# A gated MLP behind linear attention on one core: batches 0 and 1 share a tile for their last 64 positions, in a new order of steps

## The chip, the cores and the metric

The kernel runs on one core of one Trainium2 chip. The metric is device time in microseconds of one execution, taken as the median of several runs. The engines are called PE (TensorE, matmuls; PEld is its weight load), DVE (VectorE), ACT (ScalarE), POOL (GpSimd) and SP (SyncE, which here only issues loads and stores).

## What is computed

For each of 8 batches (8 heads, 576 positions, 64 channels a head) a linear attention, whose output x has 576 positions of 512 channels, and behind it a gated MLP. Cut to what matters:

```python
q_s = softmax(q, axis=-1); k_s = softmax(k, axis=2)
kv = einsum('bhsd,bhse->bhde', k_s, v)
x = einsum('bhsd,bhde->bhse', q_s, kv)          # then (b, s, 512)
h = gelu(x @ w_in)                              # 512 -> 1024
u, v = h[..., :512], h[..., 512:]
v_n = (v - mean(v)) / sqrt(var(v) + 1e-6) * g_ln
v_s = einsum('ts,bsd->btd', w_sg, v_n) + b_sg   # over the 576 positions
out = x + (u * v_s) @ w_out
```

## The kernel before, in words

Every matrix operand that meets another in the MLP is split into a high and a low part (names ending in h and l: x_h and x_l, wi_h and wi_l, ws_h and ws_l, vnh and vnl), and a product is the sum of three products of parts. One batch b passes through these steps, each a function of the kernel:

- load_q, load_k, load_v; the softmax of q (q_max, q_swapm, q_top, q_sub, q_exp, q_sum, q_swapd, q_inv, q_mul) and its transpose (q_turn); the maximum over positions of k (k_ma, k_mb, k_mc, k_fold, k_rota, k_maxa, k_rotb, k_maxb), k_sub and k_exp. Batch 0 has steps of its own for some of this (names qf_ and kr_).
- kv_mm, kv_inv, kv_scale, and x by x_mm (batch 1, line 660), xf_mm (batch 0) or xm_mm (batches 2 to 7, line 706); the copies x_high, xm_high, xt_high on ACT make the high part, x_low, xm_low, xt_low the low part. xt is the tail, the last 64 positions.
- hv_mm b i (line 773): the v half of the first layer for a tile of 128 positions, 12 matmuls of 512 columns; hv_gelu, hv_sq, hv_stat, hv_pow, hv_norm and then hv_high, hv_low give the normalized parts. i = 4 is the tail tile.
- hu_mm b f (line 843): the u half, 24 matmuls of 288 columns; hu_gelu.
- sg_mm b d (line 860): the product with w_sg, 28 matmuls of 288 columns, the last four of them with the tail (vn_1, vn_2); gate, gate_high, gate_low.
- out_mm b e: the last layer, 24 matmuls; out_base (x_h + x_l), out_add, out_store. The last one of batch 7 is done in halves (last_mm).

The 576 positions are four tiles of 128 and a tail of 64. For batches 2 to 7 an even batch and the odd one after it share one tail tile: hv_mm of the even batch with i = 4 holds both tails, and the odd batch writes its tail into the even batch's x as well (second, line 34; x_places, line 744; tail_places, line 727; tail, line 823). To have that tail in columns 0 to 63, the positions of odd batches are turned on the host so that the tail comes first, and w_sg and b_sg are laid out with 640 columns, the tail's both in front and behind; halves takes an offset (line 656 on). Batches 0 and 1 stand in ALONE (line 27): each has a tail tile of 64 positions of its own, so hv_mm 0 4 and hv_mm 1 4 both exist, each with 64 rows.

The weights are converted once at the start from raw 64-bit words: wi_a, wi_b, wi_c, wi_d, wi_h, wi_l for the eight pieces of w_in, the same with wo_ for w_out, ws_h and ws_l for w_sg, b_h and b_l for b_sg. hv_mm needs pieces 4 to 7 of w_in. Steps called warm are matmuls without use that keep PE at work at the start.

What sets the order: PLAN (line 39) is a list of all steps, written out, and the kernel runs through it once (line 921). Every engine's own instructions, SP's loads and stores among them, stay in the order of the list (InOrder, and mm for PE); across engines only data and buffers order them. A trailing V, G or A in a step says which engine does it: DVE, POOL or ACT. Buffers are slots taken in turn: two for k (kk) and q (qq), one pair for v (vv), four for v after the gelu, two banks of one kind of PSUM tile for hv_mm, kv_mm and the tails and three of a wider kind for the rest. So load_k b h can be issued once kv_mm of the batch before, same h, has read its slot, and SP's later loads and stores wait behind it.

Two quoted pieces say how x and the tail tile are addressed:

```python
def rows(b, i):
    return slice(0, TL if i == ST and b in ALONE else P)
...
        yield ps2_of(b, p)[:, :, 0:HS], split(whole(x, b)[:, p, 0:S])
        if second(b):
            yield ps2_of(b, p)[:, 0, 0:TL], x(b - 1)[:, p, S:S + TL]
```

Of the kernel before, what the change touches and what calls it, by code (L numbers as in the profile page):

```python
# [63 lines left out]
k_ma 2 1, k_mb 2 1, hv_pow 0 2, hv_high 0 2, hv_stat 0 4 A, hv_norm 0 4, hv_pow 0 4, tail_high 0, tail_again 0, ws_l 4 G, hv_stat 1 3 A, ws_h 3
k_mc 2 1, hv_mm 1 1, hv_pow 1 3, k_fold 2 1, k_rota 2 1, hv_sq 1 0, load_q 2 0, wo_h 3, load_k 2 0, q_max 2 0, q_swapm 2 0, hv_low 0 2, ws_l 3 V
tail_low 0, sg_mm 0 3, hv_gelu 1 2, k_ma 2 0, k_mb 2 0, wo_l 2 V, q_top 2 0, k_mc 2 0, k_fold 2 0, k_rota 2 0, k_maxa 2 1, k_rotb 2 1, gate 0 3
q_sub 2 0 G, hv_norm 1 3, hv_gelu 1 1 A, hv_sq 1 1, k_maxb 2 1, sg_mm 0 0, gate 0 0, wo_l 3 G, k_maxa 2 0, sg_mm 0 1, hv_stat 1 2, k_sub 2 1 V
# [4 lines left out]
q_turn 2 1, load_k 3 0, load_v 3 0, out_mm 0 1, hv_pow 1 0, kv_inv 2 1, wo_h 0, wo_l 0 G, q_sub 2 1 G, out_base 0 2 V, out_add 0 2, out_base 0 3 V
out_add 0 3, q_mul 2 0 0 G, q_turn 2 0, out_mm 0 0, q_exp 2 1, q_sum 2 1, q_swapd 2 1, out_base 0 1 G, out_add 0 1, hu_mm 1 2, k_ma 3 0, k_mb 3 0
k_mb 3 1, k_mc 3 0, q_inv 2 1, load_q 3 0, out_base 0 0 G, out_add 0 0, q_mul 2 1 1 V, out_store 0 0, hu_gelu 1 2, k_mc 3 1, hu_mm 1 3, hu_gelu 1 3
kv_scale 2 1, q_mul 2 1 0 G, q_turn 2 2, out_store 0 3, k_fold 3 0, k_rota 3 0, q_turn 2 3, xm_mm 2, k_fold 3 1, k_rota 3 1, q_max 3 0, xt_high 2
# [904 lines left out]
```

## Time and profile before

| | |
|---|---|
| median of 3 runs | 496.66 us (495.96 to 496.99) |
| profiled execution, span | 495.2 us, 9520 instructions |
| PE busy | 482.7 us, 97% |
| DVE busy | 356.0 us, 72% |
| ACT busy | 286.0 us, 58% |
| POOL busy | 177.3 us, 36% |
| HBM read, written | 37.64 MB, 9.44 MB |

The span runs from the first to the last instruction of the one execution that the profiler recorded; it is 1.46 us below the median of the runs, which were timed apart, and no other time is given for the profiled execution. The busy times are averages over stages with different limits. Nearly all operations of DVE, ACT and POOL have one line in the profile (164, the helper that keeps the order), and all matmuls have line 253, so rows are told apart by tiles, shapes and time.

### The profile page before, as it was taken

How to read it: one execution, taken by the hardware profiler on the slowest of the kernel's cores; microseconds unless marked ns; L12 is line 12 of the kernel's file. 1: busy time of each engine (PE TensorE's matmuls, PEld its weight loads, DVE VectorE, ACT ScalarE, POOL GpSimd, SP SyncE). 2: the span in 40 equal slices, each digit the busy share in tenths (PEclk: the TensorE clock that was granted, in tenths of full speed). 3: DMA queues.
4: the chain of work that ended last, by engine and by line, in shares of the span. 5: the costliest groups of instructions: out<-in, count | busy, mean ns of one | idle time of the engine just before them, and what ended most of it. 6: DMA issues, size and time to landing. Idle time of an engine off the chain costs nothing.

```text
span 495.2 us, 9520 instructions
## 1 busy us (share of the span) xinstructions
PE 482.7 (97%) x3859; PEld 444.3 (90%) x3859; DVE 356.0 (72%) x610; ACT 286.0 (58%) x603; POOL 177.3 (36%) x136
## 2 busy tenths in 40 slices
...
GB/s 316 388 396 132 190 136 1 157 141 100 1 94 207 82 16 49 107 29 116 97 66 134 119 46 34 1 72 196 8 2 1 144 73 1 1 0 49 1 1 144
DMA packets 16303, 47.68 MB, mean 96 GB/s; under 512 B 1922, under 2 KB 3332, under 8 KB 16260
## 3 DMA queue, kind: packets, MB, share of 16 engines
q1 hardware_dynamic: 16112, 47.01, 27.0%
...
HBM read 37.64 MB, written 9.44 MB: 95 GB/s over the span
## 4 chain that ended last, share of the span: by engine, by line
PE 82%; DVE 9%; DMA 3%; ACT 2%; issue 2%; SPq 1%; POOL 0%; DVEq 0%; ACTq 0%; POOLq 0%
PE ps L253 82%; DVE ot_i L164 2%; DVE km L164 1%; DMA qq<-q 1%; DVE qd L164 1%; DMA vv<-v 1%; DVE qm L164 1%; SPq L164 1%; DVE o L164 1%; DMA qq<-q_flat 1%; DVE kf L164 1%; ACT L164 1%; DVE qq L164 0%; ACT v L164 0%; POOL o L164 0%
## 5 line engine op out<-in xcount | busy, mean ns | idle before, releaser
L164 POOL TENSOR_TENSOR rs<-ve,half 128x1 f32<-128x1 f32 (+1 forms) x37 | 30.4, 826 | 101.4 <-DVE ve L164 101.4
L253 PE MATMUL ps<-ulow,wo_h 128*128 128x288 f32 x256 | 55.5, 296 | 0.0
L253 PE MATMUL ps<-gh,wo_h 128*128 128x288 f32 x256 | 55.5, 295 | 0.0
L253 PE MATMUL ps<-gh,wo_l 128*128 128x288 f32 x256 | 55.3, 295 | 0.0
L253 PE MATMUL ps<-ws_h,vnh 128*128 128x288 f32 x256 | 55.2, 297 | 0.0
L253 PE MATMUL ps<-ws_l,vnh 128*128 128x288 f32 x256 | 54.9, 296 | 0.0
L253 PE MATMUL ps<-ws_h,vnl 128*128 128x288 f32 x256 | 54.9, 296 | 0.0
L164 POOL TENSOR_TENSOR ulow<-u,gh 128x576 fp32r<-128x576 f32 x17 | 28.0, 1645 | 66.5 <-ACT gh L164 55.8
L164 POOL TENSOR_TENSOR qq<-qq,qm 128x1152 f32<-128x1152 f32 (+2 forms) x13 | 26.5, 2040 | 62.7 <-DVE qm L164 42.9
L164 ACT ACT_TABLE_LOAD x34 | 43.6, 1283 | 7.5 <-issue 3.6
L164 DVE TENSOR_TENSOR u<-ps,u 128x576 f32<-128x576 f32 x32 | 23.9, 750 | 32.8 <-PE ps L253 32.7
L164 ACT CAST gh<-u 128x576 fp32r<-128x576 f32 x32 | 21.2, 670 | 43.5 <-DVE u L164 43.5
L253 PEld LDWEIGHTS ps<-ws_h,vnh 128*128 128x128 f32 x256 | 41.5, 188 | 0.8
L253 PEld LDWEIGHTS ps<-gh,wo_h 128*128 128x128 f32 x256 | 41.3, 188 | 0.6
L253 PE MATMUL ps<-wi_h,x_h 128*128 128x512 f32 (+1 forms) x148 | 41.0, 398 | 0.7 <-DVE x_l L164 0.7
L253 PE MATMUL ps<-x_h,wi_h 128*128 128x288 f32 (+2 forms) x256 | 40.7, 299 | 0.7 <-ACT x_l L164 0.7
L253 PEld LDWEIGHTS ps<-gh,wo_l 128*128 128x128 f32 x256 | 41.3, 188 | 0.0
L253 PEld LDWEIGHTS ps<-ws_h,vnl 128*128 128x128 f32 x256 | 41.1, 188 | 0.0
L253 PEld LDWEIGHTS ps<-ulow,wo_h 128*128 128x128 f32 x256 | 41.1, 188 | 0.0
L253 PEld LDWEIGHTS ps<-ws_l,vnh 128*128 128x128 f32 x256 | 41.0, 188 | 0.0
L253 PE MATMUL ps<-wi_h,x_l 128*128 128x512 f32 (+1 forms) x148 | 40.9, 396 | 0.0
L253 PE MATMUL ps<-wi_l,x_h 128*128 128x512 f32 (+1 forms) x148 | 40.5, 395 | 0.0
...
## 6 DMA issues: line engine op xcount, KB each, us to landing
...
```

The lines of the kernel that those rows point to most:

```text
L164: ins = op(*args, **kw)
L253: tc.keep_in_program_order(nc.tensor.matmul(*args, **kw))
```

## The change

ALONE becomes empty: batches 0 and 1 share one tail tile, hv_mm 0 4 with 128 rows, and hv_mm, hv_gelu, hv_stat, hv_norm and hv_pow of 1 4 leave the plan. Batch 1 writes its tail into batch 0's x as well, so its x_high and x_low have one more copy each. The positions of odd batches keep their order, w_sg and b_sg have 576 columns, and halves loses its offset. The list of steps is in another order from end to end; 69 steps change between DVE and POOL. The number of warm steps stays eight, and no other step comes or goes (1259 steps before, 1254 after).

```diff
-WT = S + TL
+WT = S
...
-ALONE = [0, 1]
+ALONE = []
...
-    def halves(z, o=0):
-        return [z[..., o:o + HS], z[..., o + HS:o + S]]
+    def halves(z):
+        return [z[..., 0:HS], z[..., HS:S]]
...
     def main_tail(b):
-        o = second(b) * TL
-        return slice(o, o + ST * P), slice(0, TL) if o else slice(ST * P, S)
+        return slice(0, ST * P), slice(ST * P, S)
...
         if second(b):
-            yield ps2_of(b, p)[:, 0, 0:TL], x(b - 1)[:, p, S:S + TL]
+            yield ps2_of(b, p)[:, 1, HS - TL:HS], x(b - 1)[:, p, S:S + TL]
...
     def hv_mm(b, i):
-        col, n = ST * P if i == ST else second(b) * TL + i * P, rows(b, i)
+        col, n = i * P, rows(b, i)
...
     def sg_mm(b, d):
-        o, ds = TL - second(b) * TL, slice(d * P, (d + 1) * P)
+        ds = slice(d * P, (d + 1) * P)
...
-    ws = np.concatenate([ws[:, ST * P:], ws], axis=1)
```

Lines of the plan that the prediction speaks of, the old order first:

```diff
-qf_mul 0 0 0 G, qtr_mm 0 0 0, wi_b 0, qf_mul 0 0 1 G, warm 2, qf_copy 0 1 1, qf_inv 0 1 0, qf_mul 0 1 0 G, kr_exp 0 1 1, qf_copy 0 0 0, load_w_in 2
...
-wi_l 6 G, load_v 1 0, q_exp 1 0, hu_part 0 1 1, wi_h 5, b_h, kb_mm 1 1, k_sub 1 1 V, k_exp 1 1, q_sum 1 0, load_w_sg 0, hu_part 0 3 1, q_swapd 1 0
-q_sum 1 1, wi_l 4 G, kv_mm 1 0, kv_inv 1 0, kv_scale 1 0, q_inv 1 0, q_swapd 1 1, wi_l 5 G, b_l G, q_inv 1 1, hv_mm 0 0, hv_gelu 0 0 A, load_w_out 2
-hu_gpart 0 3 1, q_mul 1 0 0 V, q_mul 1 0 1 G, q_turn 1 1, q_mul 1 1 1 G, q_turn 1 0, hu_gpart 0 1 1, load_w_sg 3, hv_mm 0 3, hv_gelu 0 3 A, load_v 1 1
...
-k_rotb 2 0, k_maxb 2 0, k_sub 2 0 G, k_exp 2 1, wo_h 1, q_max 2 1, gate_high 0 0, sg_mm 0 2, wo_l 1 G, k_exp 2 0, load_v 2 1, kv_mm 2 1, load_v 2 0
-kv_mm 2 0, gate 0 1, gate_low 0 0 V, hu_mm 1 0, gate 0 2, hv_stat 1 1 A, gate_high 0 1, hv_norm 1 1, hv_pow 1 1, hv_norm 1 2, q_exp 2 0, q_sum 2 0
-kv_inv 2 0, kv_scale 2 0, gate_low 0 1 G, hv_high 1 3, load_k 3 1, gate_high 0 2, gate_low 0 2 V, hv_high 1 1, hv_low 1 1, gate_high 0 3
...
-q_max 3 1, hu_mm 1 1, k_rotb 3 1, xm_high 2 0, xm_low 2 0, load_v 3 1, q_swapm 3 1, q_top 3 1, hv_mm 1 4, hv_gelu 1 4, xm_low 2 1, hv_mm 2 3
...
-out_add 5 0, k_exp 7 1, out_mm 5 2, hu_mm 6 2, out_store 5 0, load_v 7 1, out_store 4 2, k_maxb 7 0, load_v 7 0, q_mul 7 1 0 G, q_mul 7 0 0 V
...
+load_v 0 0, kr_zero 0 1, load_w_in 1, ktr_mm 0 0, qf_inv 0 1 0, qf_mul 0 1 0 V, qf_inv 0 0 1, qf_mul 0 0 1 G, kr_copy 0 0, kr_rest 0 0, wi_a 0
...
+wi_d 4, hu_part 0 1 0, q_top 1 1, kt_mm 1 1, hu_part 0 2 0, q_sub 1 1 G, b_h, hu_gpart 0 1 0, wi_h 4, kt_mm 1 0, wi_b 5, q_max 1 0, hu_gpart 0 2 0
...
+load_w_out 2, q_swapd 1 0, hv_mm 0 0, kv_scale 1 0, q_inv 1 0, q_mul 1 0 0 V, load_w_out 1, b_l G, q_mul 1 0 1 G, hv_gelu 0 0 A, ws_h 1, q_turn 1 0
+q_swapd 1 1, q_inv 1 1, q_mul 1 1 0 G, q_mul 1 1 1 V, hu_gpart 0 1 1, hu_gpart 0 2 1, load_w_sg 3, hv_mm 0 3, ws_h 3, hu_gpart 0 3 1, hv_gelu 0 3 A
...
+kv_mm 2 1, hv_high 1 0, hv_low 1 0, out_base 0 3 V, hv_pow 1 2, kv_mm 2 0, load_k 3 1, k_ma 3 1, out_mm 0 3, q_inv 2 0, q_mul 2 0 1 G, hv_pow 1 1
...
+hv_high 1 1, out_base 1 2 G, q_turn 2 2, hv_low 1 1, k_mb 3 1, k_mc 3 1, hv_low 1 3, k_fold 3 1, k_ma 3 0, hv_low 1 2, hu_gelu 1 2
+q_swapm 3 0, q_top 3 0, xm_mm 2, tail_again 1, xm_high 2 0, sg_mm 1 0, xm_high 2 1, xt_high 2, load_q 3 1, xt_low 2, xm_low 2 0, hu_mm 1 1, q_max 3 1
...
+gate_high 5 0, hv_mm 6 1, sg_mm 5 2, load_v 7 0, hv_sq 6 3, hv_stat 6 2, hv_norm 6 3, gate_low 5 0 G, hv_stat 6 3 A, gate 5 1, gate 5 2, q_mul 7 0 0 G
```

PE's order around the joints, in the two lists: before, xm_mm 2 is followed by hu_mm 1 1, hv_mm 1 4, hv_mm 2 3, hv_mm 2 1 and sg_mm 1 2; after, by sg_mm 1 0, hu_mm 1 1 and sg_mm 1 2. Before, the last sg_mm of batch 0 is followed by kv_mm 2 1, kv_mm 2 0 and hu_mm 1 0; after, by hu_mm 1 0, kv_mm 2 1 and kv_mm 2 0.

## Rows read from the trace of the kernel before

**Rows 1.** The page's busy times (us, share of the span, instructions).
```profile
PE 482.7 (97%) x3859; PEld 444.3 (90%) x3859; DVE 356.0 (72%) x610; ACT 286.0 (58%) x603; POOL 177.3 (36%) x136
```

**Rows 2.** Busy time by stretch: length, PE, PEld, DVE, ACT, POOL (instructions), clock, DMA.
```profile
0.00:111.70 111.70, 103.97 (x875) 90.64 (x876) 103.92 (x191) 87.63 (x185) 62.99 (x57) 1.00 0.56 206
125.00:495.20 370.20, 365.44 (x2896) 343.91 (x2894) 240.26 (x401) 186.24 (x387) 110.85 (x77) 1.00 0.19 63
```

**Rows 3.** Timeline of PE: hv_mm 1 4, the step behind it, the last matmul (start, us).
```profile
117.11 1.09 PE L253 MATMUL ps<-wi_h,x_h 128*64 128x512 f32 x4
...
119.88 1.10 PE L253 MATMUL ps<-wi_h,x_h 128*128 128x512 f32 x4
120.82 1.33 PE L253 MATMUL ps<-wi_h,x_l 128*128 128x512 f32 x4
...
491.65 0.29 PE L253 MATMUL ps<-gh,wo_l 128*128 128x288 f32 x1
```

**Rows 4.** Timeline of ACT and PE, 38 to 49 us: k_exp 1 0, b_h; kv_mm 1 0, x_mm 1 0.
```profile
38.16 1.27 ACT L164 ACTIVATE kk<-kk 128x1280 f32<-128x1280 f32 x1
...
41.02 0.81 ACT L164 CAST ws<-vb 1x320 fp32r<-1x320 f32 x2
...
39.69 1.39 PE L253 MATMUL ps<-vv,kk 128*64 128x65 f32 x40
...
48.74 1.20 PE L253 MATMUL ps<-qt,kvt 64*64 64x288 f32 x16 [0.17 <-ACT u L164]
```

**Rows 5.** DVE's groups by shape: count, busy us, mean ns of one, idle before, releaser.
```profile
L164 DVE TENSOR_TENSOR qq<-qq,qm 128x640 f32<-128x640 f32 x1 | 0.8, 825 | 0.0
```

**Rows 6.** Timeline of DVE and POOL, 45 to 49 us: q_mul, three q_turn, three q_mul.
```profile
45.56 1.52 DVE L164 TENSOR_TENSOR qq<-qq,qd 128x576 f32<-128x576 f32 x1
47.00 2.08 DVE L164 STREAM_TRANSPOSE qt<-qq 128x576 f32<-128x576 f32 x3
...
45.31 3.91 POOL L164 TENSOR_TENSOR qq<-qq,qd 128x576 f32<-128x576 f32 x3 [0.61 <-DVE qd L164]
```

**Rows 7.** Timeline of PE and DVE: xm_mm 2, the first sg_mm 1, the last q_turn 2.
```profile
111.70 2.18 PE L253 MATMUL ps<-qt,kvt 64*64 64x512 f32 x32
...
125.69 0.43 PE L253 MATMUL ps<-ws_h,vnh 128*128 128x288 f32 x2
...
110.91 0.77 DVE L164 STREAM_TRANSPOSE qt<-qq 128x576 f32<-128x576 f32 x1
```

**Rows 8.** DVE's groups by shape, other forms.
```profile
L164 DVE SCALAR_TENSOR_TENSOR vnl<-v,rs,vnh 128x512 fp32r<-128x512 f32 x32 | 27.0, 857 | 8.3 <-ACT vnh L164 8.1
...
L164 DVE TENSOR_REDUCE qm<-qq 128x36 f32<-128x1152 f32 x14 | 18.8, 1341 | 1.0 <-DMA qq<-q 1.0
...
L164 DVE TENSOR_TENSOR ulow<-u,gh 128x576 fp32r<-128x576 f32 x15 | 12.4, 829 | 14.4 <-ACT gh L164 14.4
...
L164 DVE TENSOR_TENSOR km<-km 128x256 f32<-128x256 f32 x14 | 5.8, 423 | 0.3
...
L164 DVE TENSOR_TENSOR qq<-qq,qm 128x1152 f32<-128x1152 f32 x4 | 5.4, 1358 | 0.1
...
L164 DVE TENSOR_TENSOR x_l<-ps,x_h 128x128 fp32r<-128x128 f32 x18 | 4.1, 281 | 1.2 <-ACT x_h L164 1.2
```

**Rows 9.** Timeline of DVE: k_ma 3 1, and an undisturbed hv_low ahead of it.
```profile
92.07 0.75 DVE L164 SCALAR_TENSOR_TENSOR vnl<-v,rs,vnh 128x512 fp32r<-128x512 f32 x1
...
93.40 0.69 DVE L164 TENSOR_TENSOR km<-kk 128x512 f32<-128x512 f32 x1
```

**Rows 10.** Waits of PE and DVE: us in total, times, the longest.
```profile
PE ps L253 <- DMA vv<-v: 0.9, 1, 0.9
...
PE ps L253 <- DVE x_l L164: 0.7, 1, 0.7
...
DVE km L164 <- DMA kk<-k: 2.7, 2, 2.1
```

**Rows 11.** SP's issue of load_k 3 1, and landings of k in 86 to 98 us.
```profile
88.02 1.71 SPq L164 DMA_DIRECT2D kk<-k  x2
...
DMA to landing us min/median/max: 4.3/5.3/6.2
```

More of the change, by code (lines that the diff above doesn't have):

```diff
@@ L64 @@
[L64 to L67, printed above, removed]
@@ L72 @@
[L72 to L75, printed above, removed]
@@ L100 @@
-k_rota 5 0, load_q 5 0, q_max 5 0, out_mm 2 3, q_swapm 5 0, q_top 5 0, q_sub 5 0 V, hu_mm 3 3, q_exp 5 0, q_sum 5 0, load_v 5 1, k_mb 5 1, hu_gelu 3 3
-out_add 2 3, k_maxa 5 0, hv_mm 4 2, hv_gelu 4 2, out_store 2 2, out_store 2 3, hv_norm 3 2, hv_high 3 2, k_mc 5 1, k_fold 5 1, hv_mm 4 1, hv_low 3 2
-q_swapd 5 0, q_inv 5 0, q_mul 5 0 0 V, hv_gelu 4 1 A, k_rota 5 1, hu_mm 3 1, q_swapm 5 1, hu_gelu 3 1, q_top 5 1, q_sub 5 1 G, hv_mm 4 3, hv_gelu 4 3
-out_base 3 2 G, k_maxa 5 1, k_rotb 5 0, k_maxb 5 0, k_sub 5 0 G, sg_mm 3 0, gate 3 0, sg_mm 3 1, q_exp 5 1, q_sum 5 1, q_swapd 5 1, gate_high 3 0
@@ new lines @@
+load_v 4 1, hv_norm 3 1, hv_sq 3 3, k_rotb 4 0, k_mc 4 1, k_fold 4 1, hv_norm 2 2, k_rota 4 1, k_maxa 4 1, hu_mm 2 3, hu_gelu 2 3, hv_high 2 2
+hv_low 2 2, q_swapd 4 1, hv_norm 3 3, hv_gelu 3 2, hv_mm 3 0, tail_high 3, tail_low 3, q_sum 4 0, q_swapd 4 0, hu_mm 2 2, hv_stat 3 2, tail_again 2
+out_store 1 0, out_base 2 0 G, tail_low 2, hv_pow 3 2, out_base 2 2 V, q_inv 4 1, q_mul 4 1 1 V, hu_gelu 2 2, hv_gelu 3 0 A, sg_mm 2 3, sg_mm 2 2
+q_inv 4 0, q_mul 4 0 0 V, k_rotb 4 1, out_store 1 3, k_maxb 4 1, q_mul 4 0 1 G, q_turn 4 3, q_mul 4 1 0 V, sg_mm 2 0, k_maxb 4 0, gate 2 2
@@ new lines @@
+out_add 2 0, out_mm 2 1, load_k 5 1, k_ma 5 1, xm_mm 4, xm_high 4 0, hv_low 3 1, out_add 2 1, q_max 5 0, xt_high 4, load_q 5 1, out_store 2 2
+xm_low 4 0, xm_high 4 1, xm_low 4 1, out_mm 2 3, xt_low 4, q_max 5 1, out_base 3 2 V, k_mc 5 0, hv_mm 4 0, k_fold 5 0, hv_norm 3 0, k_rota 5 0
+hv_gelu 4 0 A, q_swapm 5 1, q_top 5 1, hu_mm 3 3, k_maxa 5 0, out_add 2 3, out_store 2 3, hv_low 3 3, hv_low 3 2, k_mb 5 1, q_sub 5 1 G, q_exp 5 1
+hv_pow 3 0, hv_high 3 0, out_store 2 0, hv_low 3 0, hv_sq 4 0, hv_mm 4 1, hu_gelu 3 3, hu_mm 3 1, hu_gelu 3 1, q_swapm 5 0, q_top 5 0, k_mc 5 1
@@ new lines @@
+k_fold 5 1, q_sub 5 0 V, q_sum 5 1, sg_mm 3 0, sg_mm 3 1, out_base 3 3 G, k_rotb 5 0, q_exp 5 0, q_sum 5 0, k_maxb 5 0, hv_mm 4 3, k_sub 5 0 G
+out_base 3 0 V, load_v 5 1, q_swapd 5 0, q_inv 5 0, gate 3 0, gate 3 1, hu_mm 3 2, gate_high 3 0, gate_low 3 0 G, sg_mm 3 3, k_rota 5 1, q_mul 5 0 1 G
+q_mul 5 0 0 V, k_maxa 5 1, hv_gelu 4 3, hv_stat 4 0 A, sg_mm 3 2, hu_gelu 3 2, hv_gelu 4 1 A, k_rotb 5 1, k_exp 5 0, k_maxb 5 1, q_turn 5 0
+out_store 2 1, k_sub 5 1 G, k_exp 5 1, gate_high 3 1, hv_stat 4 3, q_swapd 5 1, q_inv 5 1, gate 3 3, load_v 5 0, hv_mm 4 2, hv_gelu 4 2
```

186 lines of the change are left out of this document (93 added, 93 removed).

## The prediction

> **What bounds the kernel now.** I read the page's busy times first: PE is busy 97% of the span [rows 1]. Then the table by stretch, to see where the rest is lost. From 125 us on PE is busy 365.4 of 370.2 us, and 3.3 of the missing 4.8 lie behind its last matmul, which ends at 491.9 [rows 2, 3]; before 111.7 us DVE is as full as PE, 103.9 us each [rows 2]. So there are two regimes. Late, the end is the sum of PE's matmuls. Early, PE's queue is in order and meets inputs that DVE and ACT have only just finished, so work added to these two delays every matmul behind. The change touches both. The granted clock is 1.00 in every stretch, 2.4 GHz, so a matmul has the same price everywhere after the start.
>
> The profiled span is 495.2 us and the median of the runs 496.66. I work the sum against the span and carry the 1.46 us between them unchanged. Differences under 0.2%, 1.0 us, can't be told from none here.
>
> **What goes.** The step hv_mm 1 4 disappears, because hv_mm 0 4 now computes 128 positions instead of 64. It issued 12 matmuls, whose first starts at 117.11 and whose successor starts at 119.88 [rows 3]: 2.77 us of PE. That is 0.231 us each with 64 stationary columns; the first four of the next step, with 128, go from 119.88 to 120.82, 0.235 us each. So hv_mm 0 4 gets no dearer by its wider tile. PE was busy there and is busy behind it, so this term is real as long as PE stays the bound: **-2.8**. Also gone are one gelu, the statistics, a norm and a pow, all off PE's path.
>
> **The first stage, up to x_mm 1 0.** PE's order hardly differs there, so what counts is the work in front of two joints.
> On ACT, b_h moves ahead of k_exp 1 0 (the other exchange is one copy for another of equal length): two copies, 0.81 us [rows 4]. kv_mm 1 0 started at 39.69, only 0.26 us after k_exp 1 0 ended (38.16 + 1.27) [rows 4]. So +0.55, and up to +0.8 through wi_h 5 and wi_l 5, which follow on the same queue.
> On DVE, two multiplications come over from POOL: qf_mul 0 1 0 (128x512) and q_mul 1 1 1 (128x576). No undisturbed row has these shapes ahead of this joint; the nearest is the same kind of operation at 128x640, 0.825 us [rows 5]. By elements that is 0.66 and 0.74, together 1.4. Against it, q_mul 1 0 0 took 1.52 us, because POOL had begun its own multiplication 0.25 us earlier (45.31 against 45.56) [rows 6]; in the new order it stands directly behind q_inv 1 0 on DVE's own queue and can start first, which saves 0.8. Net +0.6, or +1.4 if nothing is saved. x_mm 1 0 started at 48.74 [rows 4], 0.35 us behind the second q_turn (two thirds of the 2.08 us from 47.00 [rows 6]), so there is next to no slack. I take **+0.9** for both causes together, since they overlap, with ends of +0.5 and +1.4.
>
> **The second stage, up to sg_mm 1 0.** Before, xm_mm 2 (111.70) was followed by hu_mm 1 1 and three hv_mm, and the first sg_mm of batch 1 started at 125.69 [rows 7]. Now sg_mm 1 0 stands right behind xm_mm 2, and hv_low 1 2 must be ready for its 15th matmul. Ahead of the last q_turn of batch 2, DVE loses two ws_l net and two gate_low (0.83 each), and six k steps of batch 3 (0.4 to 0.7 each); it gains q_max 3 0 (1.34), q_sub 2 0 (1.36), the two multiplications above, one more out_base and q_mul, and the three tail copies of x_low 1, new because batch 1 now writes its last 64 positions into batch 0's tile too [rows 8]. Such a copy is 128x64; the row for 128x128 says 0.28, so at most that. Summed, DVE has between 1.1 and 2.7 us more to do before that q_turn; I take 1.5, near the lower end, since the upper one carries means that hold POOL's blocking. The last q_turn ended at 110.91 + 0.77 = 111.68 [rows 7], so now 113.2. Behind it come three hv_low, k_mb, k_mc, k_ma and k_fold: three times 0.75 to 0.86, twice 0.42, 0.69 and twice 0.42 [rows 8, 9], less some 0.4 by which neighbours overlap, about 4.2 us. So hv_low 1 2 ends near 117.4. PE, 0.9 late, starts xm_mm 2 at 112.6, sg_mm 1 0 at 114.7 and wants hv_low 1 2 at 116.6. The wait is **+0.7**, ends 0 and +2.5. The work that used to hide this joint (11.9 us of PE) is only moved behind it, which is why a small DVE delay shows here now. sg_mm 0 stays covered: tail_low 0 has about 1.5 us more DVE work ahead but is wanted only in the 25th of 28 matmuls. The four extra ACT copies of x_high 1 hide behind hv_mm 0 1 and 0 2.
>
> **The rest.** Before, PE waited 0.7 us for an x_l and 0.9 for a load of v [rows 10]. I read the first as coming from DVE's 2.1 us wait for a k load [rows 10] that stood in SP's queue behind loads of v for batch 4, the second from load_v 7 standing behind out_store 5 0. In the new order load_q 4 1, load_q 4 0 and load_k 4 0 come ahead of load_v 4 0, and load_v 7 ahead of every store of batch 5. I expect both waits to go (-1.6) and new ones of half that size (+0.8), since every joint in the plan is tight: **-0.8**, ends -1.6 and +1.
>
> **Costed at nothing:** w_sg with 576 instead of 640 columns (5 loads, 5 copies and 5 subtractions a tenth shorter, hidden behind hv_mm; uncovered it would be a gain under 0.1 us per instruction), the positions of odd batches (the same shapes at other offsets), and the end, where the last three matmul steps only swap output columns.
>
> **Sum:** -2.8 + 0.9 + 0.7 - 0.8 = -2.0, a span of 493.2 and a time of **494.7**.
>
> **Rivals.**
> *Clean.* All four terms fall at their good ends: -2.8 + 0.5 + 0 - 1.6 = -3.9, so 492.8. For it: PE lost only about 1.6 us to waits after 125 us. Against: DVE and ACT have no slack early. Chance 0.20.
> *POOL blocks the moved multiplications.* The row shows 1.52 us for a multiplication that began while POOL ran one [rows 6]. Both moved steps now stand beside a POOL multiplication (qf_mul 0 0 0 and q_mul 1 1 0). If POOL starts first each costs 0.8 more, which adds 1.6 at x_mm 1 0: 496.3, no change to be told. For it: POOL's queue holds such work at both places. Against: q_mul 1 1 1 follows q_inv 1 1 on its own engine. Chance 0.18.
> The Trainium skill (SBUF — State Buffer, section on the two separate sides) says that GpSimd and a VectorE operation with two SBUF inputs hold one port pair as an exclusive lock for a whole instruction, whichever starts first. By that rule a block could cost a whole POOL instruction, and the trace agrees in kind. By it alone the time would be this rival's.
> *Late k loads, slower.* kv_mm 2 1 moves behind hu_mm 1 0, some 3.3 us later, and it frees the buffer of load_k 3 1. That load was issued at 88.02; now it would be at about 92.2, and landings of k there took 4.3 to 6.2 us [rows 11], so it is there at 96.5 to 98.4. DVE reached k_ma 3 1 at 93.40 [rows 9] and has some 2.5 us more in front of it now (two out_base, one q_sum, one q_sub and the moved multiplications come in, three hv_norm and two gate_low net go): 95.9. All of DVE's queue stands behind that step, the q_turns for xm_mm 2 among it. The idle is 0.6 to 2.5 us. The same arrangement returns at load_k 5 0, directly ahead of its k_ma; the like of it cost 2.1 us of DVE idle before [rows 10], of which 0.7 reached PE. With 2.5 at the first and 0.8 at the second the sum is +1.3: 498.0. It decides once the first landing comes 6.9 us or more after its issue, which would take 3.2 us. Chance 0.14.
>
> **The numbers.** The forecast has 0.48. Faster is forecast and clean case, 0.68; same is the blocked case, 0.18; slower 0.14. The range reaches from just under the clean case to short of the late loads: 492.6 to 497.6, leaving out some 0.15.
>
> **What would show it.** hv_mm 0 4 takes 2.8 us with 128 columns and batch 1 has no fifth hv_mm; x_mm 1 0 starts between 49.2 and 50.2; PE waits for vnl at sg_mm 1 0, under 1 us; no PE wait for vv at batch 7. I am wrong on the second stage if that wait is over 2 us or absent, wrong on the rest if PE's waits after 125 us pass 2 us, and wrong altogether if PE's busy time does not fall by about 2.8 us.

## The result and the profile after

The changed kernel takes 500.7 us (median of 4 runs, 500.53 to 500.95) where the kernel before takes 496.54 beside it: a ratio of 1.0083, 95% interval 1.0069 to 1.0097. It is 4.1 us slower; 494.7 was forecast. The profiled execution took 500.59 us with a span of 498.5; the span in the trace of the kernel before is 495.2, 3.3 less. The forecast carried 1.46 us around the span unchanged, but that was a median less the span of one execution. Taken run by run, the time is 1.7 to 1.9 us above the span in every later run of the kernel before, and 2.0 to 2.2 in every run of a kernel in the new order, so some 0.3 of the loss lie there; the reason is open. Three executions among the experiments took 784 to 1665 us; the ratios leave them out, and they move no median by more than 0.2.

The page's busy times answer to [rows 1]; the second line is the page's chain that ended last, as shares of the span.

```profile
PE 481.5 (97%) x3847; PEld 444.6 (89%) x3847; DVE 359.7 (72%) x618; ACT 282.6 (57%) x605; POOL 159.8 (32%) x126
...
PE 52%; DVE 18%; ACT 11%; POOL 2%; issue 2%; ACTq 0%; POOLq 0%; DVEq 0%
```

The same chain in the kernel before:

```profile
PE 82%; DVE 9%; DMA 3%; ACT 2%; issue 2%; SPq 1%; POOL 0%; DVEq 0%; ACTq 0%; POOLq 0%
```

The 12 matmuls are gone (3859 to 3847) and PE is as busy as it was, 97%. The shares of busy time show nothing of the loss. The chain shows that something changed: before, 82% of it was PE's own work; now DVE and ACT hold 29%. It is no measure of the loss, though: in the changed kernel it goes back only to 72.02 us, so that its shares add up to 85%, and in the run with the shared tile alone (below), nearly as slow, PE holds 77%. PE's busy time fell by 1.2 us and not by 2.8; records of matmuls overlap, so the start of one step to the start of the next is the better measure, and it is used below.

Busy time by stretch of the changed kernel, for [rows 2] (length, PE, PEld, DVE, ACT, POOL):

```profile
0.00:111.70 111.70, 100.99 (x848) 88.00 (x849) 101.16 (x186) 85.31 (x187) 59.44 (x54) 1.00 0.53 189
125.00:498.50 373.50, 367.69 (x2892) 345.42 (x2890) 245.42 (x413) 188.75 (x396) 98.53 (x71) 1.00 0.18 63
```

In the first 111.7 us PE and DVE have each lost some 3 us of busy time (103.97 to 100.99, 103.92 to 101.16). Both wait more: this is not one engine with more to do, but two that wait for something else. After 125 us PE is idle for 5.8 us instead of 4.8.

PE's waits, for [rows 10] (us in total, times, the longest), and then where they are, in PE's timeline (start, us, operation; in brackets the idle time before and its releaser):

```profile
PE ps L253 <- ACT kk L164: 2.1, 3, 0.9
PE ps L253 <- ACT v L164: 1.3, 1, 1.3
PE ps L253 <- DVE qt L164: 1.0, 1, 1.0
PE ps L253 <- POOL ulow L164: 0.8, 1, 0.8
PE ps L253 <- DVE o L164: 0.8, 1, 0.8
```

```profile
40.74 1.39 PE L253 MATMUL ps<-vv,kk 128*64 128x65 f32 x40 [0.71 <-ACT kk L164]
...
49.65 0.70 PE L253 MATMUL ps<-qt,kvt 64*64 64x288 f32 x2
51.32 1.20 PE L253 MATMUL ps<-qt,kvt 64*64 64x288 f32 x14 [0.97 <-DVE qt L164]
52.44 1.19 PE L253 MATMUL ps<-wi_h,x_h 128*128 128x512 f32 x4
...
77.04 1.16 PE L253 MATMUL ps<-ws,vn 128*128 128x288 f32 x4 [0.23 <-ACT kb L164]
78.04 0.43 PE L253 MATMUL ps<-ws_h,vnh 128*128 128x288 f32 x2
...
108.82 1.32 PE L253 MATMUL ps<-x_h,wi_h 128*128 128x288 f32 x8 [0.76 <-DVE o L164]
...
115.40 2.18 PE L253 MATMUL ps<-qt,kvt 64*64 64x512 f32 x32
...
120.13 0.53 PE L253 MATMUL ps<-ws_h,vnl 128*128 128x288 f32 x2 [0.49 <-DVE vnl L164]
...
151.34 0.53 PE L253 MATMUL ps<-ulow,wo_h 128*128 128x288 f32 x2 [0.85 <-POOL ulow L164]
...
268.29 0.92 PE L253 MATMUL ps<-vv,kk 128*64 128x65 f32 x24 [1.29 <-ACT v L164]
```

These are kv_mm 1 0; x_mm 1 0, stopped inside; hv_mm 0 1; the last matmuls of sg_mm 0 0, and sg_mm 0 2 behind it; hu_mm 1 3, which wants the sums that out_add 0 1 reads; xm_mm 2; sg_mm 1 0; out_mm 1 2; kv_mm 5 1. None of the waits was one of the kernel before at that place, and the two that it had late [rows 10] are gone. For the first stage, hv_mm 0 1 in PE's timeline of the kernel before:

```profile
49.87 1.19 PE L253 MATMUL ps<-wi_h,x_h 128*128 128x512 f32 x4
```

Against the forecast, term by term, in us of the span:

| term | forecast | measured | from |
|---|---|---|---|
| 12 matmuls gone | -2.8 | -2.8 issued | 3859 to 3847 |
| first stage | +0.9 | +2.6 | hv_mm 0 1 at 52.44, before 49.87 |
| second stage | +0.7 | +2.3 | sg_mm 0 0, out_mm 0 2 and sg_mm 1 0 longer than their kind by 0.9, 0.9, 0.9; 0.4 that hv_mm 1 3 lost before is gone |
| rest | -0.8 | +1.2 | out_mm 1 2, sg_mm 2 0, kv_mm 5 0 longer by 1.3, 0.4, 1.4; 0.9 and 1.0 of before gone |
| sum | -2.0 | +3.3 | 498.5 less 495.2 |

A step is set against the median of its kind in the same trace. The rows of the second stage and of the rest add up the losses that can be named; start to start the second stage comes to 2.0 and the rest to 1.5, since steps of one kind differ by some hundredths. The 12 matmuls went behind xm_mm 2, and there PE was 3.7 us late already (115.40 against 111.70 [rows 7]).

### The profile page after: what moved, and what is told of

Same layout as the page of the kernel before. It is cut to its first block, busy times and chain, and to the rows that moved or that the text cites. A ratio compares the mean times of both kernels' runs of the same rounds, so it can differ in the third digit from the quotient of the medians.

```text
span 498.5 us, 9491 instructions
## 1 busy us (share of the span) xinstructions
PE 481.5 (97%) x3847; PEld 444.6 (89%) x3847; DVE 359.7 (72%) x618; ACT 282.6 (57%) x605; POOL 159.8 (32%) x126
## 4 chain that ended last, share of the span: by engine, by line
PE 52%; DVE 18%; ACT 11%; POOL 2%; issue 2%; ACTq 0%; POOLq 0%; DVEq 0%
PE ps L253 52%; DVE qq L164 3%; DVE qd L164 3%; DVE km L164 2%; POOL kk L164 2%; DVE o L164 2%; ACT L164 2%; DVE qm L164 1%; ACT v L164 1%; DVE qt L164 1%; DVE kf L164 1%; ACT kk L164 1%; ACT ka L164 1%; ACT gh L164 1%; ACT qq L164 1%
## 5 line engine op out<-in xcount | busy, mean ns | idle before, releaser
L164 POOL TENSOR_TENSOR rs<-ve,half 128x1 f32<-128x1 f32 x36 | 29.3, 821 | 131.3 <-DVE ve L164 118.1
L164 ACT ACTIVATE u<-ps 128x576 f32<-128x576 f32 (+2 forms) x36 | 21.2, 595 | 42.7 <-PE ps L253 42.5
L164 DVE TENSOR_TENSOR o<-ps,o 128x576 f32<-128x576 f32 (+1 forms) x33 | 23.9, 732 | 23.2 <-PE ps L253 22.5
L253 PE MATMUL ps<-x_h,wi_l 128*128 128x288 f32 (+2 forms) x256 | 39.9, 296 | 0.0
L253 PE MATMUL ps<-x_l,wi_h 128*128 128x288 f32 (+2 forms) x256 | 39.8, 295 | 0.0
L253 PE MATMUL ps<-wi_h,x_h 128*128 128x512 f32 x144 | 39.5, 396 | 0.3 <-ACT wi_h L164 0.2
```

What stands on the lines that cost most here:

```text
L164: ins = op(*args, **kw)
L253: tc.keep_in_program_order(nc.tensor.matmul(*args, **kw))
```

## The experiments

Each was timed beside the kernel before on the same chip (496.2 to 496.4 there). The changed kernel is "after"; what is said to be less or more than after compares medians that were taken apart, between which the kernel before differed by up to 0.3.

**Two moves in ACT's queue.** The longest new wait is inside x_mm 1 0. Its second q_turn follows q_mul 1 1 1, which follows q_inv 1 1, and DVE waits ahead of that for ACT. ACT's timeline in after, then DVE's:

```profile
45.53 1.28 ACT L164 ACT_TABLE_LOAD   x1 [1.17 <-PE ps L253]
46.83 0.60 ACT L164 ACTIVATE v<-ps 128x512 f32<-128x512 f32 x1
...
47.55 0.66 ACT L164 CAST ws_h<-ghws 128x576 fp32r<-128x576 f32 x1
48.23 0.91 ACT L164 COPY qe<-qd 32x36 f32<-32x36 f32 x4
...
49.17 0.20 DVE L164 SCALAR_TENSOR_TENSOR qd<-qd,qe 128x36 f32<-128x36 f32 x1 [1.93 <-ACT qe L164]
```

The four copies of q_swapd 1 1 have had their input since 44.70, but in the new order they stand behind hv_gelu 0 0, which waits for PE, loads its table (1.28) and runs, and behind ws_h 1. In the order of before ws_h 1 had run at 33.28, and the copies (the last four of the eight here) stood ahead of the table load and the gelu; ACT's timeline of before:

```profile
43.15 1.85 ACT L164 COPY qe<-qd 32x36 f32<-32x36 f32 x8
45.02 1.28 ACT L164 ACT_TABLE_LOAD   x1
```

The second move is of wi_a 6, which in the new order stands behind q_swapm 1 0; DVE waits 1.3 us for it at wi_b 6.

```diff
 b_l G, q_mul 1 0 1 G,
+q_swapd 1 1,
 hv_gelu 0 0 A, ws_h 1, q_turn 1 0,
-q_swapd 1 1,
 q_inv 1 1
```

> The changed kernel with one move: the four copies of q_swapd 1 1 stand ahead of hv_gelu 0 0 in ACT's queue again, as before the change, instead of behind it and ws_h 1. Theory A (ACT's order starves DVE, and PE with it): DVE's wait of 1.9 us for qe goes, x_mm 1 0 runs through instead of stopping 1.7 us inside, and the time falls by 1.2 to 1.9 us, to about 499.0. Theory B (DVE's own work, not its idle time, sets the end of the second stage): x_mm 1 0 is earlier, but PE's waits between 73 and 122 us grow by the same amount, and the time stays within 0.5 of 500.7.

Measured: 499.51, ratio 1.0074 (1.0061 to 1.0088), 1.2 less than after by the medians. x_mm 1 0 runs through, in PE's timeline of this run:

```profile
51.37 1.20 PE L253 MATMUL ps<-qt,kvt 64*64 64x288 f32 x16
```

The interval alone does not tell this run from after (1.0069 to 1.0097): four of its six runs took 499.2 to 499.6 and two 501.0 and 501.2, one of them the profiled one. The trace does: kv_mm 1 0 starts 1.9 us later than in after (42.64 against 40.74), with the same steps ahead of it, and from there to the end of the span it is 1.3 us less (456.4 against 457.7). Theory A holds, at the low end.

```diff
 q_sub 1 1 G, b_h,
+wi_a 6,
 hu_gpart 0 1 0, wi_h 4, kt_mm 1 0, wi_b 5, q_max 1 0, hu_gpart 0 2 0, k_top 1 0, q_swapm 1 0, k_top 1 1,
-wi_a 6,
 hu_part 0 3 0
```

> The changed kernel with one other move: wi_a 6 stands behind b_h, ahead of two hu_gpart and the four copies of q_swapm 1 0, on ACT. Theory A: DVE's wait of 1.3 us ahead of wi_b 6 goes, k_exp 1 0 and kv_mm 1 0 are about 1 us earlier, and the time falls by 0.5 to 1.1, to about 499.9; it may fall by less alone, since x_mm 1 0 still waits for q_swapd 1 1, which waits for hv_gelu 0 0, but that one follows PE and so moves with it. Theory B: no change beyond 0.4 us.

Measured: 500.45 (1.0075 to 1.0101), not to be told from after.

> Both moves. Theory A: 3.2 us of DVE's idle time go, x_mm 1 0 ends 2.5 us earlier, the time is about 498.0, and if the waits at sg_mm 0 0, out_mm 0 2 and sg_mm 1 0 (0.86, 0.95 and 0.85) come from the same lateness of DVE, it is up to 0.7 less. Theory B: 500.0 to 500.7, with those three waits longer than 2.7 in sum. Theory C (the three waits have causes of their own in the new order and nothing to do with the first stage): 498.0, with the three unchanged.

Measured: 499.18, ratio 1.0058 (1.0046 to 1.0070), 1.5 less than after, and all five runs (499.05 to 499.23) lie below all of after's. Theory C is nearest: sg_mm 0 0 is 1.2 longer than its kind (0.9 in after), out_mm 0 2 and sg_mm 1 0 are unchanged, and so are the two late waits. Of the two moves nearly all comes from the first. Why the second gives so little stands in the trace of this run, ACT's timeline:

```profile
37.30 1.17 ACT L164 ACTIVATE qq<-qq 128x1152 f32<-128x1152 f32 x1
38.38 0.65 ACT L164 ACTIVATE ot_o<-raw_o_vnl 128x512 f32<-128x512 f32 x1
38.93 0.61 ACT L164 CAST wi_h<-ot_i 128x512 fp32r<-128x512 f32 x1
39.45 1.26 ACT L164 ACTIVATE kk<-kk 128x1280 f32<-128x1280 f32 x1
```

DVE's k_sub 1 0 now ends at 38.24, but k_exp 1 0 starts only at 39.45, behind q_exp 1 1, wo_a 3 and wi_h 6. DVE's wait went; the next place in ACT's queue took its stead.

**The shared tile alone.** In the first try hv_mm 0 4 moved behind the last x_low of batch 1 and all else stayed:

```diff
-ALONE = [0, 1]
+ALONE = []
...
-x_mm 1 1, x_high 1 3, hv_mm 0 4
+x_mm 1 1, x_high 1 3
...
-x_low 1 2, x_low 1 3,
+x_low 1 2, x_low 1 3, hv_mm 0 4,
...
-hv_mm 1 4, hv_gelu 1 4,
```

> The kernel before with one part of the change: the last 64 positions of batches 0 and 1 share a tile, so hv_mm 1 4 and what follows it are gone, hv_mm 0 4 moves behind the last x_low of batch 1 and does 128 positions, tail_high 1 and tail_low 1 stand beside those of batch 0. Positions of odd batches, w_sg's 640 columns and the order of all other steps are as before. If the term of -2.8 us for 12 matmuls is right and the seven more copies of tails on ACT and DVE are hidden: 493.7 to 494.3, and the new order is then worth +6.5 us. If the copies delay DVE in its full stage: 494.5 to 495.5. If PE's saved time returns as a wait: 496.5.

Measured: 502.19 (1.0107 to 1.0137), 5.9 slower than before. The place where hv_mm 0 4 had stood, between x_mm 1 1 and x_neg 1 1, now held a wait of 2.3 for x_high 1 1. Behind it the granted clock fell; PE's timeline, then a stretch of this run (length, PE, PEld, DVE, ACT, POOL, clock, DMA):

```profile
56.17 0.54 PE L253 MATMUL ps<-x_h,minus 128*128 128x288 f32 x2 [2.29 <-ACT x_h L164]
...
57.00:58.00 1.00, 1.00 (x4) 0.79 (x3) 0.97 (x2) 1.00 (x4) 0.00 (x0) 0.50 0.86 246
```

At 0.50, 1.2 GHz, hv_mm 0 2 took 4.3 us (56.54 to 60.88) where its kind takes 2.8 at 1.00, 2.4 GHz. So 1.5 of the 5.9 is the clock, and all four runs show a mean clock of 0.997. (In this order hv_gelu 0 2 also stands behind hv_mm 1 3, which overwrites the sums that it reads.) A better placement, against the kernel before, without the lines above that stay the same:

```diff
-wo_d 0, x_high 1 1, load_q 2 1
+wo_d 0, load_q 2 1
...
-x_high 1 0, x_low 1 0
+x_high 1 0, x_low 1 0, x_high 1 1
...
-x_low 1 1 A, hv_gelu 0 4 A, wo_c 2, wo_d 2, hv_pow 0 1, ws_l 2 G
-x_low 1 2, x_low 1 3
+x_low 1 1 A, x_low 1 2, x_low 1 3, hv_mm 0 4, wo_c 2, wo_d 2, hv_pow 0 1, ws_l 2 G
...
-hv_mm 1 3, hv_gelu 0 2
+hv_gelu 0 2, hv_mm 1 3, hv_gelu 0 4 A
```

> The kernel before with the shared tile alone, placed with more care than in the first try, which had taken hv_mm 0 4 away as the cover of x_high 1 1 and emitted a gelu behind the matmuls that overwrite its sums (so one tile of batch 0's v was another's there). Now x_high 1 1 stands directly behind x_low 1 0 on ACT, two x_low ahead of wo_c 2 on DVE, and hv_gelu 0 2 ahead of hv_mm 1 3. Theory D (in the first 120 us DVE sets the pace, so the 12 matmuls taken from PE come back as waits): 495.8 to 498, with new waits ahead of hv_mm 0 4, of sg_mm 0 3 or of hv_mm 2 3, where hv_mm 1 4 stood. Theory E (PE sets the pace and the term of -2.8 stands): 493.7 to 494.5.

Measured: 500.13, ratio 1.0074 (1.0060 to 1.0088), 3.9 slower than before. Theory E is out, and the loss is above D's range too. Not all of it is the tile's: two of the five runs (500.13 and 500.67) show a mean clock of 0.996, and in the profiled one (500.39, clock 1.000) kv_mm 1 0 starts at 40.86 against 39.69 [rows 4], ahead of every edit. PE's timeline of this run:

```profile
59.74 0.73 PE L253 MATMUL ps<-wi_h,x_h 128*128 128x512 f32 x2 [0.81 <-ACT x_h L164]
...
61.73 0.51 PE L253 MATMUL ps<-wi_h,x_l 128*128 128x512 f32 x1 [0.79 <-DVE x_l L164]
62.53 0.50 PE L253 MATMUL ps<-wi_h,x_l 128*128 128x512 f32 x1 [0.29 <-DVE x_l L164]
...
123.12 1.20 PE L253 MATMUL ps<-wi_h,x_h 128*128 128x512 f32 x4 [1.64 <-ACT x_h L164]
...
125.61 0.73 PE L253 MATMUL ps<-wi_h,x_l 128*128 128x512 f32 x2 [0.50 <-DVE x_l L164]
```

The first three are inside hv_mm 0 4: as a tile of 64 positions it needed batch 0 alone and gave ACT and DVE 2.8 us to finish x of batch 1; as a tile of 128 it waits for that itself. The last two are hv_mm 2 3, where hv_mm 1 4 used to stand and gave the same 2.8 us to x of batch 2. The change took away one step, and with it cover at two places.

**More and less work on PE.** In after, hv_mm 1 1, directly ahead of sg_mm 0 0, issues its 12 matmuls twice:

```diff
-        for m, (lhs, rhs, c) in enumerate(pairs):
+        for m, (lhs, rhs, c) in enumerate(pairs * (1 + ((b, i) == (1, 1)))):
```

> The changed kernel with PE's work given back: hv_mm 1 1, directly ahead of sg_mm 0 0, issues its 12 matmuls twice (2.8 us, the same sums). Theory D (DVE sets the pace up to 122 us): the waits of 0.86, 0.95 and 0.85 at sg_mm 0 0, out_mm 0 2 and sg_mm 1 0 take the added work in, and the time rises by 0 to 0.8 only, 500.7 to 501.5. Theory E (PE sets the pace): +2.8, 503.5.

Measured: 504.37 (1.0148 to 1.0179), 3.7 more than after. Both theories miss. The same kernel again, for its trace:

> A second run of hv_mm 1 1 issuing its 12 matmuls twice, for its profile; it took 504.4, 3.7 more than the changed kernel, where D expected up to 0.8 and E 2.8. Theory F: hv_gelu 1 1 comes 2.8 later, and ACT's queue behind it (k_rotb 2 0, q_swapm 2 0, both exponentials of batch 2) with it, so the waits between 73 and 122 us take nothing in, and one of them is longer. Theory E: PE has the same waits as in the changed kernel, all 2.8 later.

Measured: 504.16. The wait inside sg_mm 0 0 is gone, as theory D has it, but nothing further on takes the rest in, and a new wait comes at 280 us, inside xm_mm 5 (hu_mm 4 0 starts 3.9 us after it, 1.8 more than usual). PE's timeline of this run:

```profile
110.88 1.32 PE L253 MATMUL ps<-x_h,wi_h 128*128 128x288 f32 x8 [0.89 <-DVE o L164]
...
280.30 1.88 PE L253 MATMUL ps<-qt,kvt 64*64 64x64 f32 x20 [0.86 <-DVE kvt L164]
```

PE is 2.1 us later than in after at hu_mm 1 3 (110.88 against 108.82) and 3.6 later at the end; the reason of the late wait, which makes the difference, is open. So PE's work does count when it is added, and gelus and gates on ACT and DVE start later with it. Then the opposite, 12 fewer:

```diff
+        pairs = pairs[:6] if (b, i) in ((1, 1), (1, 2)) else pairs
         for m, (lhs, rhs, c) in enumerate(pairs):
```

> The changed kernel with 12 more matmuls taken from PE: hv_mm 1 2 and hv_mm 1 1, directly ahead of sg_mm 0 0, issue 6 of their 12 products each (the other six products are left out of these two tiles). Theory E (PE sets the pace there): -2.8, 497.9. Theory F (ACT and DVE do): 0 to -0.6, 500.1 to 500.7, with the wait inside sg_mm 0 0 grown from 0.9 to about 3.5. Gelus that start earlier could give up to -1.

Measured: 502.13 (1.0097 to 1.0125), no faster, and above the range of either theory. In the profiled execution (501.15, 0.6 above after's):

```profile
70.86 1.20 PE L253 MATMUL ps<-wi_h,x_h 128*128 128x512 f32 x4 [0.74 <-ACT v L164]
...
74.61 0.53 PE L253 MATMUL ps<-ws_h,vnl 128*128 128x288 f32 x2 [0.23 <-DVE vnl L164]
...
77.64 1.15 PE L253 MATMUL ps<-ws,vn 128*128 128x288 f32 x4 [1.20 <-ACT kb L164]
78.63 0.43 PE L253 MATMUL ps<-ws_h,vnh 128*128 128x288 f32 x2
```

sg_mm 0 2 starts at 78.63, in after at 78.04, and this run was 0.6 late at kv_mm 1 0 already (41.33 against 40.74), from waits before 16 us. So 2.8 us taken from PE moved that joint by nothing: they came back as waits of 0.74, 0.23, 1.20 and smaller ones, as theory F has it. The other three runs took 0.9 to 1.3 more than the profiled one. Two of them show a mean clock of 0.997, where the profiled one shows 1.000; for the third, also at 1.000, no trace shows the reason.

**Less work on DVE.**

```diff
-k_mb 2 1, k_mc 2 1,
...
-k_mb 2 0, k_mc 2 0,
...
+        if b == 2:
+            E.tensor_tensor(out=km_s(b, h, at=2 * b + h)[:, 0:256], in0=kk[:, 0], in1=kk[:, 1], op=ALU.max)
+            return
...
-in_=rows_of(b, h), axis=AX.X, op=ALU.max)
+in_=rows_of(b, h)[:, :, 0:8 if b == 2 else 32], axis=AX.X, op=ALU.max)
```

> The changed kernel with less work on DVE between 62 and 85 us: the maxima of batch 2, which only shift its exponentials, are taken over a part of the numbers (two of five tiles of k, 8 of 32 of q). k_mb and k_mc of both halves are left out, k_ma does 128x256 instead of 128x512, q_max 128x288 instead of 128x1152: 2 x (0.69 + 0.42 + 0.42 - 0.42) + 2 x 0.95, 4.1 us in all, 2.2 of it ahead of tail_low 0. Theory D: the three waits between 73 and 122 us shrink from 2.7 to under 0.7 and the time falls by 2.0 to 3.0, to about 498.2. Theory E: the time stays within 0.5 of 500.7. Theory C (each wait has a cause of its own on ACT or POOL): the first wait alone goes, -0.9.

Measured: 499.58, ratio 1.0067 (1.0055 to 1.0080), 1.1 less than after for 4.1 us less work: the figure of theory C, and D is out. The wait inside sg_mm 0 0 goes, the others stay. From hv_stat 0 4 (71.13) to the q_mul of 103 us, nearly every step of DVE, ACT and POOL is earlier by the same 0.87. This run's timeline of DVE, and the ACT copies it waits for:

```profile
75.09 0.17 DVE L164 TENSOR_TENSOR kf<-kf,ka 128x8 f32<-128x8 f32 x1 [1.54 <-ACT ka L164]
75.28 0.74 DVE L164 SCALAR_TENSOR_TENSOR vn<-v,rs,vn 64x512 fp32r<-64x512 f32 x1
...
74.24 0.81 ACT L164 COPY ka<-kf 32x8 f32<-32x8 f32 x4
```

tail_low 0, which sg_mm 0 0 needs, stands on DVE behind k_maxa 2 1, which waits for four small copies, which stand on ACT behind tail_high 1, ws_h 4, tail_high 0, wo_h 2 and a gelu. DVE has time to spare there in this run; ACT's queue, from 71.2 to 75.1, has none. What set that queue off is tail_high 1, which waits for hv_pow 0 4 on POOL, and that for hv_stat 0 4 on DVE, which k_mb 2 1 and k_mc 2 1, left out here, had stood directly ahead of: the chain goes through all three engines. In after it comes late: hv_stat 0 4 starts at 71.13, in the kernel before at 67.64.

**More of ACT's queue cleared.** The two moves from above and:

```diff
-wo_a 3, load_w_sg 0
+load_w_sg 0
...
+q_swapd 1 1, wo_a 3,
 hv_gelu 0 0 A
...
-ws_h 4, tail_high 0, hv_low 0 2
+ws_h 4, tail_high 0, tail_again 0, hv_low 0 2
...
-k_rota 2 1, ws_l 4 V
+k_rota 2 1, tail_low 0, ws_l 4 V
...
-k_rotb 2 0, hv_sq 1 1, q_swapm 2 0
+k_rotb 2 0, q_swapm 2 0
...
-q_swapd 2 1, q_inv 2 1, hu_gelu 1 0
+q_swapd 2 1, hv_sq 1 1, hv_stat 1 1 A, q_inv 2 1, hv_pow 1 1, hu_gelu 1 0
```

> The changed kernel with five moves in ACT's queue, two of them those of the runs before (q_swapd 1 1, wi_a 6). New: wo_a 3 goes from ahead of wi_h 6 and k_exp 1 0 to behind q_swapd 1 1; tail_again 0 directly behind tail_high 0, with tail_low 0 ahead of ws_l 4 on DVE; hv_sq 1 1 (1.06 us) from 83.7 us to behind q_swapd 2 1, its hv_stat and hv_pow with it. Theory F (up to 122 us ACT and DVE wait for each other in turn, and this chain of their queues, not DVE's amount of work, sets the time): kv_mm 1 0 is 0.6 earlier, the wait inside sg_mm 0 0 (1.16 with the first two moves) goes, what follows q_exp 2 0 is earlier by 1.0, and the time falls from 499.2 to between 497.0 and 498.2. Theory D (DVE's amount of work): under 0.5 less than 499.2, since none of DVE's work is taken away.

Measured: 498.56, ratio 1.0044 (1.0031 to 1.0056): 2.1 less than after, 0.6 less than the two moves alone, between the two theories. The waits at kv_mm 1 0 and inside sg_mm 0 0 are gone and that at hu_mm 1 3 is down to 0.45, but x_neg 1 1 starts 0.5 late, and sg_mm 1 0 waits 0.48 as ever. (The profiled run, 498.89, was also 0.6 behind after at hu_part 0 0 1, 26.70 against 26.09, before any of the moves.) The late waits are untouched.

**Two late places.**

```diff
-gate_low 1 2 G, hv_pow 2 1
+gate_low 1 2 G, gate_low 1 3 G, hv_pow 2 1
...
-out_mm 1 2, load_q 4 1
-xm_mm 3
+out_mm 1 2, out_mm 1 1, load_q 4 1
+out_add 1 2, xm_mm 3
...
-gate_low 3 0 G, sg_mm 3 3
+gate_low 3 0 G, hv_mm 4 2, sg_mm 3 3
...
-hv_gelu 4 1 A, k_rotb 5 1
+hv_gelu 4 1 A, hv_gelu 4 2, k_rotb 5 1
```

> The changed kernel with two later places put in another order. At 148 us gate_low 1 3 stands ahead of hv_pow 2 1 and q_mul 3 0 0 on POOL, and xm_mm 3 behind out_mm 1 1 on PE. At 255 us hv_mm 4 2 stands ahead of sg_mm 3 3 on PE and hv_gelu 4 2 behind hv_gelu 4 1 on ACT, so that kv_mm 5 1 does not wait for the sums that hv_gelu 4 2 reads behind a change of ACT's table. If those waits (1.35 and 1.41) come from the order alone: -2.0 to -2.8, about 498.2. If the first comes from DVE's and POOL's load, it moves to xm_mm 3 or hv_mm 2 4 and only the second goes: -1.4, 499.3.

Measured: 503.33, ratio 1.0140 (1.0126 to 1.0153), 2.6 more than after. Both waits went and others came that are larger in sum, behind xm_mm 3 and inside out_mm 3 2 (and 1.1 at xm_mm 5); three of the four runs, at 503.3 and 503.4, show a mean clock of 0.996 or 0.997, the profiled one, 502.80, shows 0.999:

```profile
158.39 1.21 PE L253 MATMUL ps<-wi_h,x_h 128*128 128x512 f32 x4 [1.92 <-DVE x_l L164]
...
271.91 0.53 PE L253 MATMUL ps<-ulow,wo_h 128*128 128x288 f32 x2 [0.72 <-DVE ulow L164]
```

hv_mm 2 2, which now follows xm_mm 3 at once, wants the sums that xt_low 3 reads. So the steps that were moved had been cover for their neighbours.

**The loads alone.** The forecast's one good term, tried on the kernel before:

```diff
-kv_scale 3 1, load_v 4 1, hv_mm 2 0
+kv_scale 3 1, load_k 4 1, hv_mm 2 0
...
-load_k 4 0, k_ma 4 0
+load_k 4 0, load_v 4 1, load_v 4 0, k_ma 4 0
...
-load_k 7 1, k_ma 7 1
+load_k 7 1, load_v 7 1, load_v 7 0, k_ma 7 1
```

> The kernel before with loads alone moved in SP's queue, as the change does in its way: load_k 4 1 ahead of hv_mm 2 0 and the loads of v for batch 4 behind load_k 4 0, and load_v 7 behind load_k 7 1 instead of behind stores of batches 4 and 5. If PE's two waits late in the kernel before (0.7 for x_l at 155 us and 0.9 for load_v 7 at 395 us) come from SP's queue, as forecast: 494.5 to 495.4, faster than both kernels. If DVE's and ACT's work behind them was as late as the loads: 496.0 to 496.5.

Measured: 495.28, ratio 0.9976 (0.9967 to 0.9985), 1.15 faster than before: the fastest kernel here. What is left of PE's waits for x_l and for loads of v, for [rows 10], in PE's timeline:

```profile
14.52 1.39 PE L253 MATMUL ps<-vv,kk 128*64 128x65 f32 x40 [0.26 <-DMA vv<-v]
...
25.50 0.86 PE L253 MATMUL ps<-x_h,wi_h 128*128 128x320 f32 x4 [0.68 <-ACT x_l L164]
```

The 0.7 for DVE's x_l at 155 us and the 0.9 for load_v 7 are gone, and PE's timeline shows no wait of 0.1 or more behind 70 us.

**Everything but the order.** The code of after with the steps of the better-placed shared tile.

> All of the change but its order: the changed kernel's code (shared tile, positions of odd batches not turned, w_sg in 576 columns) with the steps in the order of the kernel before, as in the run with the shared tile alone, which took 500.1. If the two small parts cost nothing, as forecast: 499.5 to 500.6. If the turned positions had been worth their while (xt and hv steps of odd batches read other offsets): above 500.6. If the shorter w_sg counts: down to 499.0.

Measured: 499.59, ratio 1.0055 (1.0041 to 1.0068), beside 1.0074 (1.0060 to 1.0088) for the shared tile alone. The intervals overlap: turned or not turned positions and a w_sg of 640 or 576 columns make no difference that can be told, as forecast.

## Why the prediction was wrong

**The 12 matmuls, -2.8.** Two things failed: the condition of this term, and the way in which the stages below were summed. Counted by joints, the 12 matmuls did go, and the price was right: hv_mm 0 4 with 128 columns took 2.78 us (59.73 to 62.51). The 5.3 us between forecast and result lie in the other three terms (1.7, 1.6 and 2.0). What failed here is the condition that made them a gain: "PE was busy there and is busy behind it, so this term is real as long as PE stays the bound". A full PE is no proof that PE sets the pace. In the order of before the same 12 matmuls, taken out by the shared tile alone, gave no gain but a loss, because the removed work had been cover at two places. In the new order, taking 12 more matmuls from PE gave nothing; taking 4.1 us from DVE gave 1.1; giving PE 12 back cost 3.7. The forecast looked for cover on the edits that it costed at nothing but not on the one that it took as a gain. That the wider tile makes hv_mm 0 4 depend on batch 1 was seen only as seven more copies, three of them on DVE and four on ACT. The forecast's own last sign came out against it as well: PE's busy time was to fall by about 2.8 and fell by 1.2.

**The first stage, +0.9, measured +2.6.** x_mm 1 0 did start in the forecast interval, at 49.65, and then stopped inside for 1.7. That start is luck in part: PE was 1.05 late from kv_mm 1 0 on (40.74 against 39.69), and the first q_turn lay ready since 47.24; the second, from which the forecast had worked the start out, ended at 51.26 only. "What counts is the work in front of two joints" failed: the work was summed by engine, but what ACT has in front of q_swapd 1 1 is a wait for PE. Two steps of one engine had changed places, and that cost 1.2 us (the first run). The "one copy for another of equal length" failed in the same way: ws_h 1 had run at 33.28, long before k_exp 1 0; wo_a 3, which came for it, runs at 38.24 with only wi_h 6 between it and k_exp 1 0, and makes some 0.6 of the 1.25 us by which k_exp 1 0 is late (39.41 against 38.16). b_h, which was priced, was not tried alone.

**The second stage, +0.7, measured +2.3.** The joint that was worked out came true: sg_mm 1 0 started 2.1 us behind xm_mm 2 and waited 0.49 for vnl (the forecast's own times, 117.4 and 116.6, give 0.8 and not 0.7). Both sides of it came over 2 us later than worked out: hv_low 1 2 ended at 120.08, and sg_mm 1 0 started at 117.51 instead of 114.7. But "sg_mm 0 stays covered" was wrong by 0.9, for the same reason as above (DVE's work was summed, the chain over POOL and ACT in front of k_maxa 2 1 was not looked at), and the bank of sums that hu_mm 1 3 waits for was not among the joints at all.

**The rest, -0.8, measured +1.2.** That both old waits go was right, and the loads alone show it as 1.15 us on the kernel before. "New ones of half that size" was a guess with a row for nothing but its sign: the new ones are 3.1, and PE's named waits after 125 us, 0.85, 0.19 and 1.29, pass in sum the 2 us that the forecast gave as its sign. The run with two late places shows that moving single steps does not simply take them away; what would remove them is open.

**The rivals.** Slower was given 0.14, for late k loads. That mechanism did not come: DVE waits for no load of k between 62 and 112 us, and k_ma 3 1 (99.79) follows on the step ahead of it without idle time. POOL's blocking was no part either at the moved multiplications: they took 0.69 and 0.76. It does exist further on. DVE's and POOL's timelines of after, two pairs:

```profile
49.82 0.76 DVE L164 TENSOR_TENSOR qq<-qq,qd 128x576 f32<-128x576 f32 x1
...
102.78 2.03 DVE L164 TENSOR_TENSOR qq<-qq,qd 128x576 f32<-128x576 f32 x1
```

```profile
49.86 1.73 POOL L164 TENSOR_TENSOR qq<-qq,qd 128x576 f32<-128x576 f32 x1 [2.42 <-DVE qd L164]
...
102.75 1.45 POOL L164 TENSOR_TENSOR o<-x_h,x_l 128x576 f32<-128x576 f32 x1
```

At 49.8 DVE began 0.04 ahead and took 0.76; at 102.8 it began 0.03 behind and took 1.27 more. The Trainium skill (SBUF — State Buffer, SBUF: two separate sides) says that of a GpSimd operation that reads SBUF and a VectorE operation with two SBUF inputs whichever starts first holds their shared ports for the whole instruction, and the other is blocked. Both pairs agree in who waits, by margins of 0.03 and 0.04 us; the second cost DVE 1.27 us where 1.42 of POOL's operation were left.

**Slower by how much for which part.** In the order of before the shared tile costs 3.3 to 3.9 us by the medians (2.7 to 3.7 by the ratios); the whole change costs 4.1, and 2.1 once ACT's queue is mended. The new order without the shared tile was not tried: a fifth tile of batch 1 would find no free buffer of v there until hv_low 1 3 has run, at 118.0. So it is shown that the tile's saving is lost in the order of before, and that half of the changed kernel's loss lies in the places of a few steps on ACT. It is not shown what the new order would be worth with the old tiles, nor what makes the other half: its waits can be named, but no run took them away.

## What to carry to other kernels

Before you count removed work as a gain, ask which waits it covered: look up what the next steps need, and when that was ready in the trace of before. In these queues, which keep their order, the place of a step mattered more than its length; for each joint follow back every queue that feeds it to the last step that itself waits for another engine, and see whether a step has been moved past one. A busy share of 97% on PE says nothing of this; the page's chain that ended last (82% of PE before, 52% after) is a hint to look, but no measure. A late load in a queue was the cheapest to mend here (1.15 us).

## What had not been expected

Four copies of 0.22 us on 32 partitions, moved behind one gelu, cost the whole kernel 1.2 us. In the first try of the shared tile the granted clock fell to half behind a wait of 2.3 us on PE, and that cost 1.5 more. The first loads and what follows them vary: kv_mm 0 0, with the same steps ahead of it, started at 13.05 us in after and at 14.96 in the run with q_swapd 1 1 moved, whose profiled execution took 501.15 where four of its six runs took 499.2 to 499.6.
